# A second layer's attention scores as three rounds of 32-row products, side by side in four banks

## The chip, the cores and the metric

The kernel runs on one core of one Trainium2 chip. The metric is the time of one execution on the device in microseconds (us). The core has five engines that run beside each other, each through its own instructions in order: TensorE (PE: matrix products, with weight loads shown as PEld), VectorE (DVE), ScalarE (ACT), GpSimd (POOL) and SyncE (SP, which only issues DMAs). TensorE writes its results to PSUM, eight banks of 512 float32 per partition; ScalarE and VectorE read them from there.

## The reference

Two attention layers and two gated layers, interleaved, with the same weights both times. One sequence of 2048 tokens, width 448, 16 query heads of 28 with one shared key and value head, and a gated width of 1792:

```
q = (x @ wq) in 16 heads;  k = x @ wk;  v = x @ wv          # x is layer-normalised
p = softmax(q k^T * 28 ** -0.5);  x = x + (p v, heads joined) @ wo
h = sigmoid(x @ w_gate) * (x @ w_up);  x = x + h @ w_down   # x is layer-normalised
```

These two lines of work make one layer of the kernel; there are two layers.

## The kernel before

Precision comes from splitting each float32 into a high and a low float16 part: a product is high by high plus low by high plus high by low. Tokens go in 16 units of 128 queries; keys in 16 tiles of 128 (`kt`). A step is one unit against one tile of keys, so a layer has 256 steps; the four groups of four heads (`g`) are its four score products.

The keys are stored transposed in `KK` with two halves. In the first half the rows are four blocks of 32: low, high, high, high; in the second half four copies of high (built in `kv`, turned in `kvt` or by a DMA). A query tile `QS` holds three blocks of 32 rows: high, high, low. So one product of 96 rows gives all three terms of a score (`scores`, line 584). Row 28 of the first block of `QS` holds the negated, scaled row maximum, and the key tile a constant there, so that the maximum is subtracted within the product. The exp (line 587) empties the bank into `P`.

The maxima come from an earlier pass over the high parts alone (`Maxima.step`, lines 529 to 563): a set of four `mx` products of 32 rows each, one per head, in four row groups of the array and into four banks, each emptied by a maximum on VectorE (line 554). The pass runs one unit ahead, one set per step; in the first three units of the second layer most of the sets were done earlier, and the few that remain are spread over 48 steps (`sparse`). When a unit's maxima are complete, `row_max` transposes them and a DMA writes them into `QS`.

`pv` (line 595) multiplies `P` with the values in four column groups, both for one or two steps at a time. Everything else of the layer (query projections `qp`, output `wo`, the gated layer's `gp`, `up`, `dn`) is the fill: `Filler.slice` issues fill matmuls of about a given length. The length is set so that the fill of a layer lasts to the layer's end: each step pair's share (`2 * rate`) is divided by the number of slices in the pair.

The order within a pair of steps is written out by hand in `PATHS`, one string for even `kt` and one for odd: F is a slice of fill, S one score product with its exp, M a set of `mx`, P one step's `pv`, X the issue of due side work. The second layer takes C for units 0 to 2, then D0 for even and D1 for odd units. Its D0 before is

```
"D0": ("FSFXFSSSPPM", "SSFFXSFSFM"),
```

PSUM: one bank is held by `pv`. The other seven (`BANKS`, `NBK`) are shared by `s`, `mx` and all fill tiles. A tile is given a bank when it is issued, in program order, and its first product waits until the bank's former tile has been read.

Of the kernel before, what the change touches and what calls it, by code (L numbers as in the profile page):

```python
# [8 lines left out]
F32 = mybir.dt.float32  # L9
F16 = mybir.dt.float16  # L10
I32 = mybir.dt.int32
AF = mybir.ActivationFunctionType
OP = mybir.AluOpType
# [6 lines left out]
def interleaved_layers_kernel(ctx: ExitStack, tc: tile.TileContext, x, wq, wk, wv, wo, wg, wu, wd, out, layers=2):  # L20
# [6 lines left out]
    nc = tc.nc  # L27
    _, S, D = x.shape
# [13 lines left out]
    wk1 = ctx.enter_context(tc.tile_pool(name="wk1", bufs=2))  # L42
# [316 lines left out]
    ktl = [cst.tile([128, 8, 32], F16, name=f"ktl{i}") for i in range(2)]  # L359
    for t in ktl:  # L360
        nc.vector.memset(t, 0.0)
        nc.vector.memset(t[:, 0, 28:29], 32768.0)
    KK, VV, QH = {}, {}, {}

    def layer_tiles(l):
# [5 lines left out]
    def kv(l, XT, t, kt):  # L371

        p = fps([128, 56], F32, "kv")
        yield from chain(p, lambda a, c, k: WKV[:k, a, c], lambda c, k: XT[:k, c, t * 128:(t + 1) * 128], 40, False)
        kt_ = ktl[kt % 2]

        def build():
            k = p[:, 0:28].rearrange("p (o d) -> p o d", o=1).to_broadcast([128, 7, 28])
            nc.scalar.activation(kt_[:, 1:8, 0:28], k, AF.Copy, scale=2.0 ** -18)
            nc.scalar.activation(VV[l][:, kt, 0:28], p[:, 28:56], AF.Copy, scale=2.0 ** -16)  # L380
            nc.vector.scalar_tensor_tensor(kt_[:, 0, 0:28], p[:, 0:28], 2.0 ** -18, kt_[:, 1, 0:28],
                                           op0=OP.mult, op1=OP.subtract)
        defer(build)
# [54 lines left out]
    def load_qs(l, u):  # L438
        b, t = divmod(u, 4)
        assert QDONE[l, b] == G  # L440
        q = wk1.tile([96, G, 4, 128], F16, name="QS", bufs=2)
        QS[l, u] = q
        for i, part in ((0, 0), (1, 0), (2, 1)):
            for g in range(G):
                nc.sync.dma_start(q[32 * i:32 * i + 32, g],
                                  qd[l % 2][b, g, part, :, t * 128:(t + 1) * 128].rearrange("(h d) n -> d h n", d=32))
# [118 lines left out]
    def row_max(l, u, mp, n):  # L565

        m32 = wk1.tile([128, 16], F32, name="m32")
        m16 = wk1.tile([128, 16], F16, name="m16")
        nc.vector.tensor_reduce(m32, mp.rearrange("p g h k -> p (g h) k")[:, :, :n], axis=AX.X, op=OP.max)
        nc.vector.tensor_scalar(m16, m32, -(2.0 ** -15), None, op0=OP.mult)  # L570

        def fin():
            stored.add(("m", l, u))
            p = fps([16, 128], F16, "mt")
            nc.tensor.transpose(p, m16, id16)
            r = wk1.tile([16, 128], F16, name="mr")
            nc.vector.tensor_copy(r, p)
            (nc.gpsimd if l or u else nc.sync).dma_start(QS[l, u][28:29].rearrange("o g h n -> o (g h) n"), r)
        late.append([4 if l and u in AHEAD else LT, fin, (l, u)])

    def scores(l, u, kt, g, P):
        assert ("m", l, u) in stored, (l, u, kt)
        s = psf.tile([128, 512], F32, tag=BANKS["s"], name="s", bufs=NBK[BANKS["s"]])
        nc.tensor.matmul(s, KK[l][0:96, 0, kt * 128:(kt + 1) * 128], QS[l, u][:, g].rearrange("p h n -> p (h n)"),  # L584
                         start=True, stop=True)
        p = wk1.tile([128, 512], F32, tag="P", name="P", bufs=12)
        nc.scalar.activation(p, s, AF.Exp, scale=esc)  # L587
        P.append(p)
# [259 lines left out]
    class Filler:  # L848
# [15 lines left out]
        def slice(self, ns):  # L864
            now[0] += 1
            flush()
            self.debt += ns
            for _ in range(3):
                c = next(self.first[0], None) if self.first else None
                if c is None:  # L870
                    self.first[:1] = []
                    break
                self.debt -= c
            while self.gens and self.debt > 0:
                g = self.gens[0]
                c = next(g[0], None)
                if c is None:
                    self.gens.remove(g)
                    continue
                self.debt -= c  # L880
                g[1] -= c
            if not self.gens:
                self.debt = min(self.debt, 0.0)
# [148 lines left out]
    for b in range(1, NB):  # L1032
# [8 lines left out]
        "A": ("FSFSFSFSPXM", "FSFSFSFSPXM"),  # L1041
        "B0": ("FSSFSXSPPM", "SFFSSFFSXMF"),
        "B1": ("FFSSXFSFSPMP", "SSFSFXSFM"),
        "C": ("FFSFXSSSPPM", "FSFXSSFSFM"),
        "D0": ("FSFXFSSSPPM", "SSFFXSFSFM"),
        "D1": ("FSFSXFSSPPM", "SSFFSXFSFM"),
    }

    def pair_of(l, u):
# [9 lines left out]
    for l in range(layers):  # L1059
        mx = mxs[l]  # L1060
        final = l + 1 == layers
        while late:
            late.pop(0)[1]()
        if not l:
            mx.step()
            fill.slice(0.4 * QCH)
            mx.step()
        else:
            mx.todo.sort()
            n = sum(a[0] < 4 for a in mx.todo) + 4  # L1070
            sparse = [i * (3 * KT - 1) // n for i in range(n)]
        if not final:
            layer_tiles(l + 1)
        if l:
            for b in range(2, NB):
                fill.add(qgen(l, b), G * QCH)
        flush(True)
        fill.slice((0.50 if l else 0.4) * QCH)
        waiting = []
        rate = 0.0  # L1080
        for step in range(U * KT):
            u, kt = divmod(step, KT)
            if step == HEAD and not final:
                mxs[l + 1] = Maxima(l + 1)
            P = []
            pair = pair_of(l, u)
            single = "P" in pair[0] and "P" in pair[1]
            for o in pair[kt % 2]:
                if o == "S":
                    scores(l, u, kt, len(P), P)  # L1090
                elif o == "M":
                    if l and step < 3 * KT:
                        n = step in sparse
                    else:
                        n = 1 + (u == 0 and kt in MORE)
                    if not n:
                        mx.visit()
                    for _ in range(n):
                        if not mx.step() and not final and l + 1 in mxs:
                            a = mxs[l + 1].between()  # L1100
                            if a and soon(a[0], mxs[l + 1].need(a)):
                                mxs[l + 1].step(a)
                    if kt == 2 and u + 1 < U:
                        load_qs(l, u + 1)
                elif o == "P":
                    for _ in range(len(waiting) if single else min(1, len(waiting))):
                        pv(*waiting.pop(0))
                elif o == "X":
                    if u and kt == 1:
                        b = (u - 1) // TB  # L1110
                        if (l, b) not in BLK:
                            BLK[l, b] = Block(l, b)
                        later(*BLK[l, b].tile(u - 1))
                    if l == 0:
                        paced(step)
                    tick()
                    fed = sum(BLK[l, b].fed == TB for b in range(NBL) if (l, b) in BLK)
                    if fed < NBL - 1:
                        rate = fill.left / max(FIRST + TB * KT * fed - step, 1)
                    else:  # L1120
                        rate = max(fill.left - KEEP, 0) / (U * KT - step)
                else:
                    fill.slice(2 * rate / "".join(pair).count("F"))
            waiting.append((l, u, kt, P))
        while waiting:
            pv(*waiting.pop(0))
        flush(True)
        later(*BLK[l, NBL - 1].tile(U - 1))
        n = 0
        nx = None if final else mxs[l + 1]  # L1130
        while side or pend or (fill.gens if final else not nx.started()):
            tick()
            for _ in range(0 if fine else 2):
                fill.slice(VS / 2)
            n += 1
            a = None if final else nx.between()
            if a:
                kz = nx.need(a)
                if soon(a[0], kz):
                    go = n >= 2 and not fine  # L1140
                elif kz == S - 128:
                    go = len(fine) > 1
                else:
                    go = True
                if go:
                    nx.step(a)
                    n = 0
            for _ in range(4 if fine else 0):
                fill.slice(VS / 4)
        if not final:  # L1150
            fill.slice(QCH)
# [21 lines left out]
```

## Time and profile before

| | us |
|---|---|
| median of 2 runs | 2256.29 (2255.59 to 2256.99) |
| the profiled execution | 2255.21 |
| its span, first to last instruction | 2253.2 |
| scores of the first layer, first to last | 87.6 to 1106.3 |
| scores of the second layer, first to last | 1226.2 to 2165.8 |
| mean granted TensorE clock | 0.997 of full |

Rows of groups read: line, engine, operation, out<-in, shapes, count, then busy time and mean ns of one, then the engine's idle time ahead of them and what ended it. Rows of a timeline read: start, length, engine, line, what, and in brackets idle time ahead. Matmuls are pipelined, so the length of one is longer than the distance to the next start, and it is the distances that count. In the profile a `pv` product in float32 shows as two instructions.

### The profile page before, as it was taken

What the parts mean: (1) busy time and instruction counts of PE and PEld (TensorE: products, weight loads), DVE (VectorE), ACT (ScalarE), POOL (GpSimd) and SP (SyncE); (2) the same over time, 40 slices, a digit from 0 to 9 for tenths busy, and PEclk for the clock granted to TensorE, in tenths of its full rate; (3) what the DMA queues carried; (4) which work ended last, traced back from release to release, by engine and by line L of the source; (5) the groups of instructions that cost most, each with busy time, mean ns of one, the idle gap of its engine ahead of it and who ended that gap; (6) DMA issues with size and microseconds to landing.
All of it is one profiled execution on the core that took longest, in us unless ns stands there. A gap on an engine that the chain in (4) does not pass through costs nothing.

```text
span 2253.2 us, 41480 instructions
## 1 busy us (share of the span) xinstructions
PE 2200.9 (98%) x15915; PEld 1029.9 (46%) x15915; DVE 1640.0 (73%) x2905; ACT 1546.2 (69%) x2595; POOL 337.5 (15%) x590
## 2 busy tenths in 40 slices
PE   8999999999999999999998999999999999999999
PEld 3322344444544444454563324445454544445467
DVE  7988887877777787777786557777777877777322
ACT  5798776776667677676514997777676767777741
POOL 5114773101110110001011011000000000000010
PEclk9999999999999999999999999999999999999999
DMA  4333662423313142332441123233231323223233
GB/s 142 106 110 92 205 214 59 118 66 89 113 60 103 56 113 76 98 106 56 129 135 35 36 64 97 77 88 98 67 102 56 93 64 102 76 88 96 70 110 119
DMA packets 203622, 213.28 MB, mean 95 GB/s; under 512 B 135376, under 2 KB 164240, under 8 KB 203424
## 3 DMA queue, kind: packets, MB, share of 16 engines
q1 hardware_dynamic: 198080, 195.78, 29.1%
q0 software_dynamic: 5344, 14.87, 1.9%
q8 instruction: 124, 2.03, 0.4%
q14 instruction: 74, 0.61, 0.1%
HBM read 175.37 MB, written 23.59 MB: 88 GB/s over the span
## 4 chain that ended last, share of the span: by engine, by line
PE 86%; DVE 7%; ACT 2%; DMA 2%; issue 1%; POOL 1%; SPq 1%; DVEq 0%; ACTq 0%; POOLq 0%
PE pv L595 20%; PE s L584 19%; PE up L352 12%; PE gp L352 11%; PE dn L784 11%; PE mx L549 7%; DVE mp L554 5%; PE wo L695 3%; PE qp L352 2%; ACT P L587 1%; DMA rgu<-in_B_w_up_dram 0%; DMA sums<-rc 0%; DMA rq<-in_A_wq_dram 0%; PE hot L916 0%; DVE sgu L131 0%
## 5 line engine op out<-in xcount | busy, mean ns | idle before, releaser
L587 ACT ACTIVATE P<-s,esc 128x512 f32<-128x512 f32 x2048 | 1295.5, 690 | 483.3 <-PE s L584 470.7
L554 DVE TENSOR_REDUCE mp<-mx 128x1 f32<-128x512 f32 x2048 | 1270.0, 683 | 394.6 <-PE mx L549 390.3
L584 PE MATMUL s<-QS,KK 96*128 96x512 f16 x2048 | 684.1, 381 | 20.0 <-DVE mp L554 12.6
L352 PEld LDWEIGHTS <-wgu 128*128 128x128 f16 x4928 | 467.6, 97 | 191.2 <-issue 49.6
L595 PE MATMUL pv<-P,VV 128*32 128x512 f32 x4096 | 509.0, 600 | 0.0
L352 PE MATMUL gp<-XT,wgu 128*128 128x256 f16 x2464 | 349.4, 272 | 0.9 <-DVE mp L554 0.7
L352 PE MATMUL up<-XT,wgu 128*128 128x256 f16 x2464 | 346.0, 272 | 1.9 <-DVE mp L554 1.2
L784 PE MATMUL dn<-WD,h 128*128 128x448 f16 x1344 | 298.5, 352 | 0.0
L584 PEld LDWEIGHTS <-KK 96*128 96x128 f16 x2048 | 186.6, 98 | 200.0 <-issue 113.0
L595 PEld LDWEIGHTS pv<-P,VV 128*32 128x32 f32 x4096 | 98.6, 108 | 239.0 <-issue 236.9
L549 PE MATMUL mx<-KK,QH 32*128 32x512 f16 x1792 | 187.5, 385 | 4.0 <-DVE mp L554 2.0
L784 PEld LDWEIGHTS <-h 128*128 128x128 f16 x1344 | 127.0, 97 | 131.6 <-issue 13.5
L549 PEld LDWEIGHTS <-QH 32*128 32x128 f16 x1792 | 46.1, 91 | 257.8 <-issue 253.9
L669 POOL TENSOR_TENSOR lb<-pvs,lb 128x512 f32<-128x512 f32 x32 | 40.4, 1264 | 728.1 <-DMA lb<-sums 647.9
L352 PE MATMUL qp<-XT,WQ 128*128 128x512 f16 x352 | 115.0, 394 | 1.1 <-DVE mp L554 0.4
L754 DVE SCALAR_TENSOR_TENSOR th<-th,up 128x512 f32<-128x512 f32 x112 | 76.3, 682 | 49.0 <-PE up L352 43.5
L306 POOL TENSOR_SCALAR rs<-mv 128x1 f32<-128x1 f32 (+1 forms) x50 | 11.2, 225 | 672.6 <-DVE mv L291 604.1
L757 ACT ACTIVATE h<-th 128x512 f16<-128x512 f32 x112 | 70.5, 629 | 52.7 <-DVE th L754 52.6
L746 ACT ACTIVATE th<-gp,gsc 128x512 f32<-128x512 f32 x112 | 77.1, 688 | 37.8 <-PE gp L352 37.5
L758 DVE SCALAR_TENSOR_TENSOR h<-th,h 128x512 f16<-128x512 f32 x112 | 76.9, 687 | 21.7 <-ACT h L757 21.7
L695 PE MATMUL wo<-WO,oT 128*128 128x448 f16 x384 | 90.7, 353 | 0.2 <-ACT P L587 0.2
L352 PEld LDWEIGHTS <-WQ 128*128 128x128 f16 x352 | 34.0, 100 | 59.6 <-issue 36.0
(151 smaller groups left out, 915.5 us busy)
## 6 DMA issues: line engine op xcount, KB each, us to landing
wgu<-wgu_d SPq DMA_DIRECT2D x224, 512.0 KB
QS<-qd SPq DMA_DIRECT2D x384, 32.0 KB
lb<-sums SPq DMA_DIRECT2D x128, 64.0 KB
xr<-in_A_x_dram SPq DMA_DIRECT2D x32, 224.0 KB
qd<-qst POOLq DMA_DIRECT2D x28, 256.0 KB, 2.7
wgu_d<-sgu POOLq DMA_DIRECT2D x14, 512.0 KB, 3.7
x2d<-x SPq DMA_DIRECT2D x16, 224.0 KB
xr<-x2d SPq DMA_DIRECT2D x16, 224.0 KB
```

What stands on the lines that cost most here:

```text
L352: nc.tensor.matmul(ps, a, b, start=n == 0, stop=n == 10)
L549: nc.tensor.matmul(ps[h][:, i * w:(i + 1) * w], qh[32 * h:32 * h + 32, g], KK[l][32 * h:32 * h + 32, 1, ka:kz], start=True, stop=True, til ...
L554: nc.vector.tensor_reduce(o, ps[h].rearrange("p (g k) -> p g k", g=n), axis=AX.X, op=OP.max)
L584: nc.tensor.matmul(s, KK[l][0:96, 0, kt * 128:(kt + 1) * 128], QS[l, u][:, g].rearrange("p h n -> p (h n)"), start=True, stop=True)
L587: nc.scalar.activation(p, s, AF.Exp, scale=esc)
L595: nc.tensor.matmul(v[32 * g:32 * g + 32], VV[l][:, kt], P[g], start=kt == 0, stop=kt == KT - 1, tile_position=(0, 32 * g))
L695: nc.tensor.matmul(p, v["oT"][:, a, h * 128:(h + 1) * 128], WO[:, c, h], start=n == 0, stop=n == 11)
L746: defer(lambda: nc.scalar.activation(th, gp.rearrange("p j n -> p (j n)"), AF.Tanh, scale=gsc))
L754: nc.vector.scalar_tensor_tensor(t, th, 1.0, up.rearrange("p j n -> p (j n)"), op0=OP.add, op1=OP.mult)
L757: nc.scalar.activation(h[:, 0], t, AF.Copy, scale=2.0 ** -17)
L758: defer(lambda: nc.vector.scalar_tensor_tensor(h[:, 1], t, 2.0 ** -17, h[:, 0], op0=OP.mult, op1=OP.subtract), 2)
L784: nc.tensor.matmul(p, hs[f // 2][:, a, o:o + 128], WD[:, f, c], start=n == 0, stop=n == 3 * FC - 1)
```

## The change

In the second layer only, the four score products of a step become one block (`Y` in the paths). Key rows now hold four copies of low in the first half of `KK` and four of high in the second. A query tile holds head group `g` in rows 32g to 32g+31, its high part and its low part behind each other. `block` takes four banks and issues twelve products of 32 rows and 512 columns in three rounds: low key by high query, high by high, high by low, each round with the four groups in four row groups of the array, each group adding in its own bank. The four exps follow. The maxima go to `QS` by four DMAs instead of one, the query tile is loaded by eight DMAs instead of twelve, and one `mx` set fewer is spread over the first three units (`+ 3` for `+ 4`).

```diff
-        nc.vector.memset(t[:, 0, 28:29], 32768.0)
+        nc.vector.memset(t[:, 0:4, 28:29], 32768.0)
...
-            nc.scalar.activation(kt_[:, 1:8, 0:28], k, AF.Copy, scale=2.0 ** -18)
+            nc.scalar.activation(kt_[:, 4 if l else 1:8, 0:28], k[:, 0:4] if l else k, AF.Copy, scale=2.0 ** -18)
             nc.scalar.activation(VV[l][:, kt, 0:28], p[:, 28:56], AF.Copy, scale=2.0 ** -16)
+            if l:
+                nc.vector.scalar_tensor_tensor(kt_[:, 0:4, 0:28], k[:, 0:4], 2.0 ** -18, kt_[:, 4:8, 0:28],
+                                               op0=OP.mult, op1=OP.subtract)
+                return
...
-        q = wk1.tile([96, G, 4, 128], F16, name="QS", bufs=2)
+        q = wk1.tile([128, G, 4, 128], F16, name="QS", bufs=2)
         QS[l, u] = q
+        if l:
+            for i in range(2):
+                for g in range(G):
+                    nc.sync.dma_start(q[32 * g:32 * g + 32, i],
+                                      qd[l % 2][b, g, i, :, t * 128:(t + 1) * 128].rearrange("(h d) n -> d h n", d=32))
+            return
...
+            if l:
+                for g in range(G):
+                    nc.gpsimd.dma_start(QS[l, u][32 * g + 28:32 * g + 29, 0], r[4 * g:4 * g + 4])
+                return
...
+    def block(l, u, kt, P):
+        assert ("m", l, u) in stored, (l, u, kt)
+        q, k = QS[l, u].rearrange("p i h n -> p i (h n)"), KK[l][:, :, kt * 128:(kt + 1) * 128]
+        s = [psf.tile([128, 512], F32, tag=BANKS["s"], name="s", bufs=NBK[BANKS["s"]]) for _ in range(G)]
+        for n, (a, c) in enumerate(((0, 0), (1, 0), (1, 1))):
+            for g in range(G):
+                r = slice(32 * g, 32 * g + 32)
+                nc.tensor.matmul(s[g], k[r, a], q[r, c], start=n == 0, stop=n == 2, tile_position=(32 * g, 0))
+        for g in range(G):
+            p = wk1.tile([128, 512], F32, tag="P", name="P", bufs=12)
+            nc.scalar.activation(p, s[g], AF.Exp, scale=esc)
+            P.append(p)
...
-        "C": ("FFSFXSSSPPM", "FSFXSSFSFM"),
-        "D0": ("FSFXFSSSPPM", "SSFFXSFSFM"),
-        "D1": ("FSFSXFSSPPM", "SSFFSXFSFM"),
+        "C": ("FXFFYPPMF", "FXFYFFFM"),
+        "D0": ("FFFXYPPMFF", "FYFFXFM"),
+        "D1": ("FFXFFYPPM", "FFFXYFFFM"),
...
-            n = sum(a[0] < 4 for a in mx.todo) + 4
+            n = sum(a[0] < 4 for a in mx.todo) + 3
...
-                if o == "S":
+                if o == "Y":
+                    block(l, u, kt, P)
+                elif o == "S":
```

What this does to the order is seen at three places. First, TensorE in the middle of the second layer, at the end of an even step. Before, the last three scores, `pv` and a set of `mx` stand there; the names in brackets are the counters waited for, of VectorE (DVE_49) and of ScalarE (Activation_49), which show who must have emptied the bank.

```order
L584 MATMUL s<-QS,KK 128x512 [waits DVE_49]
L584 LDWEIGHTS KK
L584 MATMUL s<-QS,KK 128x512 [waits DVE_49]
L595 MATMUL pv<-P,VV 32x512 x8
L549 LDWEIGHTS QH
L549 MATMUL mx<-KK,QH 128x512 [waits Activation_49]
L549 LDWEIGHTS QH
L549 MATMUL mx<-KK,QH 128x512 [waits DVE_49]
L549 LDWEIGHTS QH
L549 MATMUL mx<-KK,QH 128x512 [waits Activation_49]
L549 LDWEIGHTS QH
L549 MATMUL mx<-KK,QH 128x512 [waits DVE_49]
```

The same place now, from the last two products of the block's third round on:

```order
L602 MATMUL s<-QS,KK 128x512
L602 LDWEIGHTS KK
L602 MATMUL s<-QS,KK 128x512
L622 MATMUL pv<-P,VV 32x512 x8
L559 LDWEIGHTS QH
L559 MATMUL mx<-KK,QH 128x512 [waits DVE_49]
L559 LDWEIGHTS QH
L559 MATMUL mx<-KK,QH 128x512 [waits DVE_49]
L559 LDWEIGHTS QH
L559 MATMUL mx<-KK,QH 128x512 [waits Activation_49]
L559 LDWEIGHTS QH
L559 MATMUL mx<-KK,QH 128x512 [waits Activation_49]
```

The two banks that the set takes from ScalarE are now banks of the block that stands right ahead of it. Second, TensorE at the beginning of a step. Before, single scores stand between pieces of fill (here the output product `wo`), after a set of `mx`:

```order
L549 LDWEIGHTS QH
L549 MATMUL mx<-KK,QH 128x512 [waits Activation_49]
L695 LDWEIGHTS oT
L695 MATMUL wo<-WO,oT 128x448
L695 LDWEIGHTS oT
L695 MATMUL wo<-WO,oT 128x448
L695 LDWEIGHTS oT
L695 MATMUL wo<-WO,oT 128x448
L584 LDWEIGHTS KK
L584 MATMUL s<-QS,KK 128x512 [waits Activation_49]
```

Now the whole first round of the block stands there, after ten matmuls of fill (the last is shown) that follow the set of `mx`:

```order
L352 LDWEIGHTS wgu
L352 MATMUL up<-XT_20843,wgu 128x256
L602 LDWEIGHTS KK
L602 MATMUL s<-QS,KK 128x512 [waits Activation_49]
L602 LDWEIGHTS KK [waits PE_49]
L602 MATMUL s<-QS,KK 128x512 [waits Activation_49]
L602 LDWEIGHTS KK
L602 MATMUL s<-QS,KK 128x512 [waits DVE_49]
L602 LDWEIGHTS KK
L602 MATMUL s<-QS,KK 128x512 [waits DVE_49]
L602 LDWEIGHTS KK
L602 MATMUL s<-QS,KK 128x512
```

The block's last two banks are those of the first two products of the `mx` set ahead of it. Third, ScalarE in the second layer. Before, `th` and `h` of the gated layer stand between exps of one to three scores:

```order
L587 ACTIVATE P<-s,esc 128x512 [waits PE_49]
L587 ACTIVATE P<-s,esc 128x512 [waits PE_49,Activation_49] x2
L587 ACTIVATE P<-s,esc 128x512 [waits PE_49] x2
L746 ACTIVATE th<-gp,gsc 128x512 [waits PE_49]
L587 ACTIVATE P<-s,esc 128x512 [waits PE_49,Activation_49]
L587 ACTIVATE P<-s,esc 128x512 [waits PE_49] x3
L587 ACTIVATE P<-s,esc 128x512 [waits PE_49,Activation_49]
```

Now exps stand in runs of four, and `th` and `h` between blocks:

```order
L773 ACTIVATE th<-gp,gsc 128x512 [waits PE_49]
L605 ACTIVATE P<-s,esc 128x512 [waits PE_49,Activation_49] x8
L784 ACTIVATE h<-th 128x512 [waits DVE_49]
L773 ACTIVATE th<-gp,gsc 128x512 [waits PE_49]
L605 ACTIVATE P<-s,esc 128x512 [waits PE_49,Activation_49] x8
```

The count of exps and of maxima is the same as before.

More of the change, by code (lines that the diff above doesn't have):

```diff
@@ L583, in scores @@
         s = psf.tile([128, 512], F32, tag=BANKS["s"], name="s", bufs=NBK[BANKS["s"]])
-        nc.tensor.matmul(s, KK[l][0:96, 0, kt * 128:(kt + 1) * 128], QS[l, u][:, g].rearrange("p h n -> p (h n)"),
+        nc.tensor.matmul(s, KK[l][0:96, 0, kt * 128:(kt + 1) * 128], QS[l, u][0:96, g].rearrange("p h n -> p (h n)"),
                          start=True, stop=True)
```

## The prediction

> **What bounds the kernel now.** I read the page first: busy time of each engine, then the chain that ended last.
>
> ```profile
> PE 2200.9 (98%) x15915; PEld 1029.9 (46%) x15915; DVE 1640.0 (73%) x2905; ACT 1546.2 (69%) x2595; POOL 337.5 (15%) x590
> ...
> PE 86%; DVE 7%; ACT 2%; DMA 2%; issue 1%; POOL 1%; SPq 1%; DVEq 0%; ACTq 0%; POOLq 0%
> ...
> L587 ACT ACTIVATE P<-s,esc 128x512 f32<-128x512 f32 x2048 | 1295.5, 690 | 483.3 <-PE s L584 470.7
> L554 DVE TENSOR_REDUCE mp<-mx 128x1 f32<-128x512 f32 x2048 | 1270.0, 683 | 394.6 <-PE mx L549 390.3
> L584 PE MATMUL s<-QS,KK 96*128 96x512 f16 x2048 | 684.1, 381 | 20.0 <-DVE mp L554 12.6
> ```
>
> TensorE is never idle for long and is 86% of the chain. The other two large consumers empty its PSUM banks: ScalarE takes an exp from each score bank, VectorE a maximum from each `mx` bank. They wait for TensorE (470.7 and 390.3 us), while the scores wait for banks for only 20.0 us in the whole run. Next, the second layer alone by windows:
>
> ```profile
> 1226.20:2165.80 939.60, 933.73 (x6713) 429.93 (x6714) 646.40 (x1105) 712.25 (x1152) 74.54 (x158) 1.00 0.26 79
> ...
> 1500.00:1650.00 150.00, 149.62 (x1112) 71.88 (x1109) 114.98 (x196) 109.02 (x174) 10.81 (x23) 1.00 0.27 83
> ```
>
> The columns are the length, then busy time of PE, PEld, DVE, ACT, POOL, then granted clock. PE is busy 149.6 of 150 us at full clock, while DVE and ACT have a quarter of their time left. On this reading less PE work is a shorter layer, as long as banks keep coming free. So I read two steps in order of time, PE first, then ACT and DVE.
>
> ```profile
> 1500.22 0.40 PE L549 MATMUL mx<-KK,QH 32*128 32x512 f16 x4
> 1500.55 0.61 PE L584 MATMUL s<-QS,KK 96*128 96x512 f16 x2
> 1500.99 1.04 PE L352 MATMUL gp<-XT,wgu 128*128 128x256 f16 x8
> 1501.87 0.38 PE L584 MATMUL s<-QS,KK 96*128 96x512 f16 x1
> 1502.09 0.60 PE L352 MATMUL gp<-XT,wgu 128*128 128x256 f16 x4
> 1502.52 0.38 PE L584 MATMUL s<-QS,KK 96*128 96x512 f16 x1
> 1502.74 0.60 PE L352 MATMUL gp<-XT,wgu 128*128 128x256 f16 x4
> 1503.28 0.40 PE L549 MATMUL mx<-KK,QH 32*128 32x512 f16 x4
> 1503.60 0.61 PE L352 MATMUL gp<-XT,wgu 128*128 128x256 f16 x4
> 1504.05 0.38 PE L584 MATMUL s<-QS,KK 96*128 96x512 f16 x1
> 1504.27 0.27 PE L352 MATMUL gp<-XT,wgu 128*128 128x256 f16 x1
> 1504.38 0.49 PE L352 MATMUL up<-XT,wgu 128*128 128x256 f16 x3
> 1504.71 0.38 PE L584 MATMUL s<-QS,KK 96*128 96x512 f16 x1
> 1504.93 0.60 PE L352 MATMUL up<-XT,wgu 128*128 128x256 f16 x4
> 1505.36 0.60 PE L584 MATMUL s<-QS,KK 96*128 96x512 f16 x2
> 1505.89 1.92 PE L595 MATMUL pv<-P,VV 128*32 128x512 f32 x16
> 1507.75 0.39 PE L549 MATMUL mx<-KK,QH 32*128 32x512 f16 x4
> ```
>
> ```profile
> 1504.47 0.69 ACT L587 ACTIVATE P<-s,esc 128x512 f32<-128x512 f32 x1 [0.34 <-PE s L584]
> 1505.05 0.68 ACT L746 ACTIVATE th<-gp,gsc 128x512 f32<-128x512 f32 x1
> 1505.62 1.84 ACT L587 ACTIVATE P<-s,esc 128x512 f32<-128x512 f32 x3
> ```
>
> ```profile
> 1500.64 2.48 DVE L554 TENSOR_REDUCE mp<-mx 128x1 f32<-128x512 f32 x4 [1.39 <-PE mx L549]
> ```
>
> From one start to the next this prices everything. A pair of steps is 1500.22 to 1507.75, 7.53 us. A score product is (1500.99 - 1500.55) / 2 = 0.22, a fill matmul (1501.87 - 1500.99) / 8 = 0.11, and the pair holds 28 of them, 3.08 us. Changing how the array is split costs: the four fill matmuls ahead of `mx` take 0.54 instead of 0.44, so entering row groups is 0.10; the two scores ahead of `pv` take 0.53, so entering column groups is 0.09; the two `pv` take 1.86 with leaving. A set of four `mx` holds the array 0.33 before the next work starts. How much of that is leaving, and whether further rounds in the same row groups need their weights waited for, is shown where sets were cut into narrower products:
>
> ```profile
> 1212.73 0.40 PE L549 MATMUL mx<-KK,QHB 32*128 32x128 f16 x16
> 1213.07 1.11 PE L352 MATMUL qp<-XT,WQ 128*128 128x512 f16 x3
> ...
> 1173.33 0.40 PE L549 MATMUL mx<-KK,QHB 32*128 32x256 f16 x8
> 1173.66 0.72 PE L352 MATMUL up<-XT,wgu 128*128 128x256 f16 x5
> ```
>
> Four rounds of 128 columns (0.34), two of 256 (0.33) and one of 512 (0.33) hold the array equally long. So rounds follow each other at the pace of their columns, weight loads hidden: a round of 512 is 0.22, leaving is 0.11.
>
> For the banks: an exp starts 0.42 after its product (1504.05 to 1504.47), a first maximum 0.42 after its `mx` (1500.22 to 1500.64). Three exps run in 1.84, so (1.84 - 0.69) / 2 = 0.575 apart; four maxima in 2.48, so (2.48 - 0.68) / 3 = 0.60 apart. After the last round of four products that end together, the second and third bank are free at 0.42 + 0.575 + 0.69 = 1.69 and 2.26; after a set of `mx`, at 0.42 + 0.60 + 0.68 = 1.70 and 2.30.
>
> **Part 1: the products themselves.** Per step four scores of 0.22 (0.88) become three rounds of 0.22 (0.66): -0.44 per pair. In the even step, entering and leaving row groups (0.21) replaces entering `pv` from full width (0.09): +0.12. In the odd step both are new: +0.21. Net -0.11 per pair, and 128 pairs give **-14 us**. Leaving row groups straight into `pv` is not in the trace; I take the 0.11 seen towards full width. Between nothing and twice that, the term moves 14 us either way.
>
> **Part 2: when the banks come free.** Scores, `mx` and fill share seven banks. Before, the score products are spread over the step and each has its exp behind it within about 0.4 us. Now a block needs four banks at once, and none has its result until the third round; then four exps queue. A block, a set of `mx` and one or two fill tiles make nine or ten tiles for seven banks, so each set takes two or three banks from the set just before it. I counted this from the banks that the built program assigns: of 210 times that `mx` follows a block, the last bank needed is the second exp's 165 times and the third's 45 times; of 211 blocks after `mx`, the second maximum's 143 times and the third's 68 times. The waits in the order above say the same: two of four wait for ScalarE, two for VectorE.
>
> What lies between is too short. A pair has 3.08 us of fill in nine slices (units 0 to 2 and even units) or eleven (odd ones): 0.34 or 0.28 each. From the start of a set's last round to the next set is 0.22 + 0.11 + the slices + 0.10:
> - odd step, block to `mx`: three slices, 1.45 or 1.27, mean 1.36. Short of 1.69 by 0.33, of 2.26 by 0.90; weighted 79 to 21: 0.45.
> - even step, block to `mx`: 0.22 + 0.11 + 1.86 = 2.19; short only of 2.26: 0.02.
> - even step's `mx` to the next block: three slices, 1.36; short of 1.70 by 0.34, of 2.30 by 0.94; weighted 68 to 32: 0.53.
> - odd step's `mx` to the next block: 1.5, plus what `mx` itself waited (its first two products run at once and their maxima go ahead): at least 1.83, short only of 2.30: 0.13.
>
> Together 1.13 us per pair in which TensorE stands, with fill, `pv` and all else queued behind it in order. About 210 steps have a set of `mx` (the first three units have few, the last none), so 105 pairs: **+119 us**. The waits that are there now are too few to return much: they are in the 20.0 us above.
>
> **Part 3: other work in the two queues.** `th` (row 1505.05) and `h` stand between the exps, `th` and `h` again between the maxima, 56 each in this layer. Hidden now; one in four ahead of a needed bank, half of it (0.3) exposed, is 224 / 4 x 0.3 = **+17 us**, an estimate from those rows, with 0 and 60 as ends.
>
> **Part 4: what is hidden.** Query loads go from twelve to eight per unit; SyncE needs 5.73 us for twelve and loads a unit ahead, so fewer gain nothing. The row of maxima goes in four DMAs on GpSimd, not one:
>
> ```profile
> 1678.56 5.73 SPq L445 DMA_DIRECT2D QS<-qd  x12
> ```
>
> ```profile
> L578 POOL DMA_DIRECT2D QS<-mr x31: 522/606/637, 136.4 to 2100.7; - x31
> ...
> DMA to landing us min/median/max: 1.6/1.7/5.2
> ```
>
> Four issues of 0.61 and 1.7 to land are 4.1 us, 1.8 more. One sparse `mx` set fewer lets them start three steps ahead of the unit instead of four; two steps, 7.4 us, remain after the transpose. Without that cover it is under 2 us for each of 15 units. The low key part is now built four times, 16 times in all:
>
> ```profile
> L381 DVE SCALAR_TENSOR_TENSOR ktl<-kv,ktl x32: 174/184/189, 18.8 to 1216.9; 128x28 f16<-128x28 f32 x32
> ```
>
> At most four times 0.18, so 0 to 9 us on VectorE, between the layers, mostly beside fill; I take nothing, as ScalarE's copy ahead of it shrinks.
>
> **Sum.** -14 + 119 + 17 = +122. The profiled execution took 2255.2 us, 1.1 under the median of the runs, so 2256.3 + 122 = 2378 us.
>
> **Rivals.**
> 1. *Banks in time* (the other side). If exps and maxima keep ahead, only part 1 is left: 2242, and 2222 with the 20.0 us of waits gone too. It holds if a block and its `mx` are 1.69 us apart, 0.33 more than counted. For it: both engines have a quarter of their time left. Against: it isn't their load but four results ending together. Over 2% faster (under 2211) would need the mode changes to be free as well: 0.44 x 128 = 56 us, 2200.
> 2. *Rounds dearer than their columns.* If weights of a row group cannot load while it computes, two further rounds a step each wait for a load, 98 ns:
>
> ```profile
> L584 PEld LDWEIGHTS <-KK 96*128 96x128 f16 x2048 | 186.6, 98 | 200.0 <-issue 113.0
> ```
>
> That is 0.20 x 256 = +51, 2429. Against it are the rows with 16 and 8 products. The Trainium skill ("TensorE: Matmul & The Clock Gate", Part 3 on packing small matmuls) says that a weight load overlaps matmuls in flight only where the row group differs, and gives 3.07x for four row groups at 512 columns. By that ratio a round is 0.88 / 3.07 = 0.29, an estimate from that page: 0.86 per block, part 1 becomes +37 and the sum again 2429. This case's trace does not agree: 0.33 with one, two or four rounds.
> 3. *Waits relieve each other.* A wait at `mx` gives the maxima and fill evictions time, so only half of part 2 is left: -14 + 60 = 2302; a little more relief is within 2%.
> 4. *Not side by side.* If products into four banks with sums run one after another, a block is 12 x 0.22 = 2.64: +1.76 x 256 = 450, 2706. `mx` already runs four row groups into four banks, though without adding.
>
> **Chances.** Forecast 0.70; rival 1: 0.11 (0.03 of it under 2211); rival 2: 0.09; rival 3: 0.08; rival 4: 0.02. A measurement tells about 2%, 45 us. Range: from rival 3's 2300 to 2440, which takes in rival 2, part 3's upper end and part 1's. Slower by over 2% are the forecast, rivals 2 and 4 and half of rival 3: 0.85; faster 0.03; within 0.12.
>
> **What would show it.** Right: idle time of PE ahead of `s` and `mx` in the second layer of some 130 us, ended by VectorE's maxima for `s` and by the exps for `mx`; the layer's windows showing PE at about 90% instead of 99.7%; a block's three rounds holding the array 0.66 and 0.1 for each change. Wrong: sets of `mx` that start on time in odd steps, a block over 0.9 us without a wait, or waits on GpSimd's DMAs at a unit's start. The first layer should be unchanged.

## The result and the profile after

The changed kernel takes 2373.8 us (2373.19 to 2374.41, 2 runs) against 2256.29: a ratio of 1.0523, 95% interval 1.0497 to 1.0549. It is 5% slower. The page of the changed kernel, with the engines, the chain of waits, and the groups of the block's products, the `mx` sets, and the first layer's scores:

```profile
PE 2288.7 (97%) x17963; PEld 1008.5 (43%) x17963; DVE 1643.3 (69%) x2905; ACT 1519.6 (64%) x2595; POOL 362.5 (15%) x638
...
PE 79%; DVE 10%; ACT 5%; issue 3%; DMA 1%; POOL 1%; SPq 0%; ACTq 0%; DVEq 0%; POOLq 0%
...
L611 PE MATMUL s<-QS,KK 96*128 96x512 f16 x1024 | 348.7, 381 | 17.1 <-DVE mp L564 11.1
...
L602 PE MATMUL s<-QS,KK 32*128 32x512 f16 x3072 | 291.1, 381 | 24.6 <-DVE mp L564 16.8
...
L559 PE MATMUL mx<-KK,QH 32*128 32x512 f16 x1792 | 209.9, 384 | 9.1 <-ACT P L605 4.3
```

At first sight TensorE is as busy as before, 97% against 98%, and idle ahead of the blocks for only 24.6 us. The chain tells more: TensorE's share fell from 86% to 79%, and VectorE and ScalarE together went from 9% to 15%. The view of the scores gives first and last start of each layer's products:

```profile
L602 PE MATMUL s<-QS,KK x3072: 371/374/630, 1231.0 to 2282.8; 32*128 32x512 f16 x192
L611 PE MATMUL s<-QS,KK x1024: 376/381/634, 89.0 to 1110.4; 96*128 96x512 f16 x171
```

The first layer takes 1021.4 us (1018.7 before), the second 1051.8 instead of 939.6. So 112.2 of the 118.2 us by which the span grew lie in the second layer's 256 steps. A pair of its steps in order of time, PE and then DVE and ACT:

```profile
1704.20 0.39 PE L559 MATMUL mx<-KK,QH 32*128 32x512 f16 x4
1704.53 1.05 PE L352 MATMUL up<-XT,wgu 128*128 128x256 f16 x8
1705.50 1.26 PE L602 MATMUL s<-QS,KK 32*128 32x512 f16 x12
1706.70 1.16 PE L352 MATMUL up<-XT,wgu 128*128 128x256 f16 x9
1707.79 0.57 PE L559 MATMUL mx<-KK,QH 32*128 32x512 f16 x4
1708.29 0.50 PE L352 MATMUL up<-XT,wgu 128*128 128x256 f16 x3
1708.62 1.15 PE L352 MATMUL gp<-XT,wgu 128*128 128x256 f16 x9
1709.70 1.25 PE L602 MATMUL s<-QS,KK 32*128 32x512 f16 x12
1710.88 1.92 PE L622 MATMUL pv<-P,VV 128*32 128x512 f32 x16
1712.74 0.39 PE L559 MATMUL mx<-KK,QH 32*128 32x512 f16 x4
```

```profile
1704.62 2.48 DVE L564 TENSOR_REDUCE mp<-mx 128x1 f32<-128x512 f32 x4 [1.87 <-PE mx L559]
1708.21 2.48 DVE L564 TENSOR_REDUCE mp<-mx 128x1 f32<-128x512 f32 x4 [1.10 <-PE mx L559]
```

```profile
1706.67 2.42 ACT L605 ACTIVATE P<-s,esc 128x512 f32<-128x512 f32 x4 [1.94 <-PE s L602]
1708.96 0.63 ACT L702 CAST oT<-lb 128x512 f16<-128x512 f32 x1
1710.85 2.42 ACT L605 ACTIVATE P<-s,esc 128x512 f32<-128x512 f32 x4 [1.26 <-PE s L602]
```

The pair takes 1704.20 to 1712.74, 8.54 us against 7.53. A block that waits for nothing holds the array 0.76 us, from its first start to the next work's (all 16 blocks of the last unit, which has no sets of `mx`). Here the two blocks hold it 1706.70 - 1705.50 = 1.20 and 1.18, and the odd step's `mx` holds it 1708.29 - 1707.79 = 0.50 instead of 0.33. The wait stands inside the set: the first products start at once, the last one or two when their banks are free, and the next rounds queue behind them. With 1704.20 as the start of `mx` and maxima from 1704.62, the second maximum ends at 1704.62 + 0.60 + 0.68 = 1705.90; the fourth product of the block starts at 1705.96 in the trace. The second block needs the third maximum of the next set, which ends at 1708.21 + 2 x 0.60 + 0.68 = 1710.09; its fourth product starts at 1710.15 in the trace.

This holds beyond one pair. I laid the banks that the built program assigns beside the trace: of 223 sets and blocks in units 3 to 14 that wait more than 0.05 us, 220 start their fourth product 0.05 to 0.11 us after an exp or a maximum has emptied one of their four banks, the last one to come free.

As the wait stands inside the set, the page hardly shows it as idle time: a product's record is 0.37 to 0.39 us long, and the three that started keep the engine busy on paper. So below I give, from the starts of all second-layer matmuls of a trace, the time from the first to the fourth product of each block and set, summed. Unhindered it is 0.01 us. A block counts as even when `pv` follows it, a set when `pv` stands ahead of it. "Rest" is the layer's length (first to last score product) without these waits.

| run | second layer | blocks, odd step | blocks, even | `mx`, odd | `mx`, even | sum of waits | rest |
|---|---|---|---|---|---|---|---|
| changed kernel | 1051.8 | 57.1 | 48.7 | 38.6 | 3.1 | 147.5 | 904 |
| maxima halved | 995.8 | 14.6 | 22.9 | 51.3 | 2.3 | 91.1 | 905 |
| exps halved | 1021.7 | 59.3 | 50.5 | 10.3 | 1.1 | 121.2 | 901 |
| both halved | 948.3 | 16.5 | 14.2 | 14.5 | 1.1 | 46.2 | 902 |
| six banks | 1200.7 | 110.9 | 63.0 | 87.4 | 12.3 | 273.5 | 927 |
| one round | 935.2 | 55.0 | 47.8 | 24.5 | 3.6 | 130.9 | 804 |

In the kernel before, the `mx` sets' sum is 3.8 us and its scores are single products.

### The profile page after: what moved, and what is told of

It reads as the page before. It is cut to its first block, busy times and chain, and to the rows that moved or that the text cites. A ratio compares the mean times of both kernels' runs of the same rounds, so it can differ in the third digit from the quotient of the medians.

```text
span 2371.4 us, 46157 instructions
## 1 busy us (share of the span) xinstructions
PE 2288.7 (97%) x17963; PEld 1008.5 (43%) x17963; DVE 1643.3 (69%) x2905; ACT 1519.6 (64%) x2595; POOL 362.5 (15%) x638
## 4 chain that ended last, share of the span: by engine, by line
PE 79%; DVE 10%; ACT 5%; issue 3%; DMA 1%; POOL 1%; SPq 0%; ACTq 0%; DVEq 0%; POOLq 0%
PE pv L622 19%; PE up L352 10%; PE gp L352 10%; PE dn L811 10%; PE s L602 9%; PE s L611 9%; DVE mp L564 8%; PE mx L559 7%; ACT P L605 3%; PE wo L722 3%; PE qp L352 2%; ACT P L614 1%; DVE sgu L131 0%; DMA sums<-rc 0%; DMA rq<-in_A_wq_dram 0%
## 5 line engine op out<-in xcount | busy, mean ns | idle before, releaser
L605 ACT ACTIVATE P<-s,esc 128x512 f32<-128x512 f32 x1024 | 618.8, 689 | 365.2 <-PE s L602 364.9
L614 ACT ACTIVATE P<-s,esc 128x512 f32<-128x512 f32 x1024 | 644.2, 691 | 262.7 <-PE s L611 259.3
L352 PEld LDWEIGHTS <-wgu 128*128 128x128 f16 x4928 | 457.3, 98 | 207.8 <-issue 113.7
L611 PE MATMUL s<-QS,KK 96*128 96x512 f16 x1024 | 348.7, 381 | 17.1 <-DVE mp L564 11.1
L352 PE MATMUL gp<-XT,wgu 128*128 128x256 f16 x2464 | 335.4, 273 | 1.1 <-DVE mp L564 0.7
L352 PE MATMUL up<-XT,wgu 128*128 128x256 f16 x2464 | 332.4, 273 | 0.9 <-ACT P L614 0.9
L602 PE MATMUL s<-QS,KK 32*128 32x512 f16 x3072 | 291.1, 381 | 24.6 <-DVE mp L564 16.8
L811 PE MATMUL dn<-WD,h 128*128 128x448 f16 x1344 | 291.3, 353 | 0.0
L559 PE MATMUL mx<-KK,QH 32*128 32x512 f16 x1792 | 209.9, 384 | 9.1 <-ACT P L605 4.3
L602 PEld LDWEIGHTS <-KK 32*128 32x128 f16 x3072 | 81.4, 92 | 180.1 <-issue 146.2
L611 PEld LDWEIGHTS <-KK 96*128 96x128 f16 x1024 | 95.7, 98 | 111.0 <-issue 70.3
L306 POOL TENSOR_SCALAR rs<-mv 128x1 f32<-128x1 f32 (+1 forms) x50 | 11.3, 226 | 747.6 <-DVE mv L291 740.3
L784 ACT ACTIVATE h<-th 128x512 f16<-128x512 f32 x112 | 71.2, 636 | 57.1 <-DVE th L781 57.0
L773 ACT ACTIVATE th<-gp,gsc 128x512 f32<-128x512 f32 x112 | 77.7, 694 | 41.7 <-PE gp L352 41.4
```

The costliest lines, as they stand in the source:

```text
L352: nc.tensor.matmul(ps, a, b, start=n == 0, stop=n == 10)
L559: nc.tensor.matmul(ps[h][:, i * w:(i + 1) * w], qh[32 * h:32 * h + 32, g], KK[l][32 * h:32 * h + 32, 1, ka:kz], start=True, stop=True, til ...
L602: nc.tensor.matmul(s[g], k[r, a], q[r, c], start=n == 0, stop=n == 2, tile_position=(32 * g, 0))
L605: nc.scalar.activation(p, s[g], AF.Exp, scale=esc)
L773: defer(lambda: nc.scalar.activation(th, gp.rearrange("p j n -> p (j n)"), AF.Tanh, scale=gsc))
L784: nc.scalar.activation(h[:, 0], t, AF.Copy, scale=2.0 ** -17)
```

## The experiments

Four experiments have a ratio, from four to ten runs; the other five are one run each. Runs of the kernel before, repeated beside them, lie between 2254.98 and 2263.35 us.

**Four full-height products in the block's place.** The kernel before with the new places of work:

```diff
-        "D0": ("FSFXFSSSPPM", "SSFFXSFSFM"),
+        "D0": ("FFFXSSSSPPMFF", "FSSSSFFXFM"),
...
-            n = sum(a[0] < 4 for a in mx.todo) + 4
+            n = sum(a[0] < 4 for a in mx.todo) + 3
```

> The kernel before with the new order of work: where the new paths have a block, four score products of 96 rows stand one after another (0.88 us), all else as before. Theory (banks are late because the four results of a block end together): here the first exp starts 0.66 us ahead of the fourth product, so counted from the last product the second bank is free after 1.03 us instead of 1.69, and the last product of the four comes 0.66 us later for the maxima. Sets of mx should hardly wait, products wait only for a third maximum (about 0.1 us per pair): 2256 to 2285 us. Rival (the places of the work in the step are at fault, whatever the products): it stays within 20 us of 2374. Rival (32-row rounds or changes of the array's split are dear): 2256, no waits.

Measured 2285.35 us, ratio 1.0119 (1.0097 to 1.0141): at the upper edge of the theory's range, and 88 us below the changed kernel. Its second layer takes 968.7 us. Sets of `mx` wait 16.5 us in sum, and single products wait more than I expected, for maxima. In order of time:

```profile
1643.15 0.60 PE L352 MATMUL gp<-XT,wgu 128*128 128x256 f16 x4
1643.59 0.82 PE L584 MATMUL s<-QS,KK 96*128 96x512 f16 x3
1644.63 0.38 PE L584 MATMUL s<-QS,KK 96*128 96x512 f16 x1 [0.22 <-DVE mp L554]
1644.85 1.04 PE L352 MATMUL gp<-XT,wgu 128*128 128x256 f16 x8
1645.81 0.40 PE L549 MATMUL mx<-KK,QH 32*128 32x512 f16 x4
```

The fourth product should start 0.66 us after the first, at 1644.25; it starts at 1644.63. So the places alone cost 29 us of the 118, and the form of the products, with results that end together, costs the other 88 or so. The rival that blames the places alone, with a time near 2374, falls; a quarter of the loss is theirs all the same.

**Maxima halved.** Of the changed kernel, the second layer's maxima read half of each bank:

```diff
-                nc.vector.tensor_reduce(o, ps[h].rearrange("p (g k) -> p g k", g=n), axis=AX.X, op=OP.max)
+                src = ps[h].rearrange("p (g k) -> p g k", g=n)
+                nc.vector.tensor_reduce(o, src[:, :, 0:w // 2] if l else src, axis=AX.X, op=OP.max)
```

> The changed kernel, but in the second layer each maximum reads only half of the columns of its bank (leaves out half of the keys in the maxima). A maximum should take about 0.36 us instead of 0.68. Theory (banks): the second and third maximum end 1.1 and 1.4 us after their set, under the 1.36 us that lie between, so blocks in steps with a set ahead stop waiting (their waits sum to about 63 us in the steady units of the changed kernel), while sets of mx wait as before or more (26 us there), and blocks of the first three units, which wait for exps, keep theirs: 2285 to 2325 us. Rival (array: rounds and changes of split are dear): within 10 us of 2374. Rival (ScalarE's load is the limit): within 20 us of 2374.

Measured 2305.84 us, in the theory's range; neither rival fits. Groups of its maxima, whole and halved:

```profile
L565 DVE TENSOR_REDUCE mp<-mx 128x1 f32<-128x512 f32 x1024 | 634.0, 682 | 153.4 <-PE mx L559 151.0
L565 DVE TENSOR_REDUCE mp<-mx 128x1 f32<-128x256 f32 x1008 | 358.8, 417 | 512.8 <-PE mx L559 510.8
```

With 417 ns instead of 682 the blocks' waits fall from 105.8 to 37.5 us, and those of `mx` rise from 41.7 to 53.7. I take the rise to come from blocks that no longer wait and so end sooner before the set, while the exps take as long as before.

**Exps halved.** The other side; `pv` reads the half twice and costs TensorE the same:

```diff
-            nc.scalar.activation(p, s[g], AF.Exp, scale=esc)
+            nc.scalar.activation(p[:, 0:256], s[g][:, 0:256], AF.Exp, scale=esc)
...
+            x = P[g][:, 0:256].rearrange("p (o n) -> p o n", o=1).to_broadcast([128, 2, 256]) if l else P[g]
...
```

> The changed kernel, but in the second layer each exp reads and writes only half of its bank, and pv reads that half twice, so that TensorE has the same work (leaves out half of the queries' scores). An exp should take about 0.36 us. Theory (banks): sets of mx in odd steps stop waiting (26 us in the steady units, 13 us in the first three), blocks of the first three units, which wait for exps, too (about 40 us); blocks in steady units still wait for maxima, a little more than now (63 to 85 us): 2290 to 2325 us. Rival (array): within 10 us of 2374. Rival (VectorE's load is the limit): within 30 us of 2374.

Measured 2339.99 us, 15 us above the range. The waits of `mx` go as expected (41.7 to 11.3 us), and the blocks' waits in units 3 to 14 grow (70.7 to 82.8 us). What I had wrong were the first three units: their blocks' waits only fall from 35.0 to 26.8 us. I had taken them for waits for exps, but in the changed kernel the delays within these blocks end 17.3 us with an exp and 16.9 us with a maximum; here it is 6.6 and 19.6 us. The chains of this run and of the one before it, in the middle of the second layer, show what each halving leaves (first this run, with halved exps):

```profile
by line: PE pv L623 21.7%; PE s L602 20.5%; DVE mp L564 14.2%; PE dn L812 11.1%; PE up L352 10.1%; PE gp L352 8.5%; PE mx L559 8.3%; PE wo L723 3.0%; issue 1.9%; PE mt L585 0.2%; DVE h L786 0.2%; ACT P L605 0.2%; DVE oT L704 0.1%; ACT h L78
```

The run with halved maxima:

```profile
by line: PE pv L623 22.5%; PE s L603 19.9%; PE up L352 12.5%; PE gp L352 11.8%; PE dn L812 11.5%; PE mx L559 9.7%; ACT P L606 5.8%; PE wo L723 3.3%; issue 2.5%; ACTq L606 0.2%; DVE h L786 0.1%; ACT h L785 0.1%; DVE mp L565 0.0%; ACTq L703 0
```

The maxima (`mp`) stand at 14.2% and 0.0%, the exps (`P`) at 0.2% and 5.8%. In the changed kernel they are 9.9% and 5.0%, in the kernel before the maxima are 1.9% and the exps under 0.1%:

```profile
by line: PE pv L622 21.4%; PE s L602 20.3%; DVE mp L564 9.9%; PE up L352 9.8%; PE gp L352 9.7%; PE dn L811 9.0%; PE mx L559 8.5%; ACT P L605 5.0%; issue 3.4%; PE wo L722 2.5%; DVE h L785 0.2%; ACTq L605 0.1%; DVE oT L703 0.1%; ACT h L784 0.
```

```profile
by line: PE pv L595 23.7%; PE s L584 22.6%; PE gp L352 14.0%; PE up L352 14.0%; PE dn L784 11.8%; PE mx L549 8.3%; PE wo L695 2.7%; DVE mp L554 1.9%; issue 0.5%; PE qp L352 0.4%; PE mt L575 0.1%
```

**Both halved, in both kernels.** The edits above together, in the changed kernel and, with the same meaning, in the kernel before.

> The changed kernel with both halvings in the second layer: maxima read half of a bank, exps read and write half of it, pv reads that half twice (leaves out half of the keys in the maxima and half of the scores). TensorE's work and order are those of the changed kernel. Theory (banks): with 0.42 us maxima and 0.48 us exps the second and third bank are free within 1.36 us, so nearly all of the 147 us of waits in blocks and sets go, and what is left is the products: 2235 to 2255 us, within 15 us of the kernel before with the same two halvings. Rival (array: rounds or changes of split cost more than counted): 2270 us or more, and over 20 us above the kernel before with the halvings.

> The kernel before with the same two halvings in its second layer (leaves out the same parts). Its scores hardly wait for banks there, so it should gain only the 15 to 23 us of small waits of its second layer: 2232 to 2245 us. The difference to the changed kernel with the halvings is what the products alone bring: -14 us was predicted, -20 to +10 expected here, as some waits of the first three units may stay. If the engines' load had been the limit of the kernel before, it would fall by more than 40 us.

Measured 2262.15 us for the changed kernel so altered, ratio to the kernel before 1.0016 (1.0007 to 1.0026), and 2236.37 for the kernel before so altered, 0.9898 (0.988 to 0.9916). The second is in its range, and as it gains only some 20 us, the load of VectorE and ScalarE was not what held the kernel before. The first is 7 us over its own range, and 26 us over the second where I expected 10 at most. That meets one of the two signs that I had named for dear rounds (over 20 us above), not the other (2270 or more). The table says what the 26 us are: 46.2 us of waits are left, 25.8 of them in the first 220 us of the layer. Where nothing waits, the products are cheaper as counted; in order of time:

```profile
1643.05 0.83 PE L603 MATMUL s<-QS,KK 32*128 32x512 f16 x12
1643.80 1.16 PE L352 MATMUL up<-XT,wgu 128*128 128x256 f16 x9
1644.89 0.40 PE L559 MATMUL mx<-KK,QH 32*128 32x512 f16 x4
1645.22 0.50 PE L352 MATMUL up<-XT,wgu 128*128 128x256 f16 x3
```

The block holds the array 0.75 us here with its exit, and `mx` 0.33. The second layer of the kernel before with the halvings is 926.5 us; some 10 us of that, an estimate good to a few us, is time by which starts come later than usual for their kind, which leaves some 916. The changed kernel's "rest" is 901 to 905 in four runs. So the products and changes of split alone bring about 12 us, and the rival that called them dear falls by the "rest" and the 0.75 us of a block, although the time came nearer to its bound than I expected.

**Six banks instead of seven**, in both kernels:

```diff
-    NBK = {"f": 7, "s": 2, "m": 3}
+    NBK = {"f": 6, "s": 2, "m": 3}
```

> The changed kernel with six shared banks in place of seven. Theory (banks): each set then takes one more bank from the set just ahead of it, one more exp (0.575 us) or maximum (0.60 us): the four waits of a pair grow by some 1.6 us together, 105 pairs: 2500 to 2580 us. Rival (array, or the order of work): under 2400 us. The first layer's and the time between the layers grow as they do in the kernel before with six banks.

> The kernel before with six shared banks in place of seven. Theory: its single scores free their banks one by one, so the lost bank costs its second layer much less than it costs the changed kernel's: under 60 us in the second layer against 120 us or more there; the whole 2290 to 2390 us. Rival (both kernels live off the seventh bank alike): the same loss in both second layers.

Measured 2603.97 and 2420.95 us, both above their ranges. The first layer, equal in both, loses 80.2 and 75.8 us, which I had left too small in both expectations. The second layer loses 148.9 us in the changed kernel (1051.8 to 1200.7) and 84.8 in the kernel before (939.6 to 1024.4), where I expected under 60. The direction is the theory's, the ratio smaller than I had it: the kernel before also lives off its seventh bank. In the changed kernel 126 of the 149 us are in the sets and blocks: 273.5 us of waits instead of 147.5. The other 23 are in the "rest", and may be the clock: it was granted at 0.50 for 60 us of this layer, against 14 us in the changed kernel, which is worth up to (60 - 14) / 2 = 23 us.

**One round only.** Two of the three rounds left out:

```diff
-        for n, (a, c) in enumerate(((0, 0), (1, 0), (1, 1))):
+        for n, (a, c) in enumerate(((0, 0),)):
```

> The changed kernel with only the first of the three rounds of a block (leaves out two of the three terms of the second layer's scores). Theory (banks): the time from a block's last round to the next set is the same, so the waits stay about as they are (some 145 us in sets and blocks), and the layer is shorter by two rounds, 0.43 x 256 = 110 us: 2250 to 2275 us. Rival (rounds are dearer than 0.215 us each, weights not loaded ahead): a fall of 130 us or more, to 2244 or less. Rival (the engines' load per step sets the pace): waits grow by what the rounds give, and the time stays over 2330 us.

Measured 2252.25 us, in the theory's range. The rest of the layer falls by 904 - 804 = 100 us, 0.20 us for each of 512 rounds left out, and a block of the last unit holds the array 0.33 us instead of 0.76, 0.215 per round. One score product of the same 512 columns holds it 0.22 in the kernel before, so a further round is not dearer than its columns. The waits stay near: 130.9 instead of 147.5.

**The same work spread evenly.** The changed kernel with other places in units 3 to 15:

```diff
-        "D0": ("FFFXYPPMFF", "FYFFXFM"),
-        "D1": ("FFXFFYPPM", "FFFXYFFFM"),
+        "D0": ("FFFFXYPFMPF", "YFFXFFM"),
+        "D1": ("FFFFXYPFMPF", "YFFXFFM"),
```

> The changed kernel with the same work put in other places in units 3 to 15 of the second layer: even step FFFFXYPFMPF, odd step YFFXFFM, so that all four distances between a block and a set are about 1.67 us instead of 1.36, 2.19, 1.36 and 1.5, for one more entry into and exit from column groups per pair (0.21 us). Theory (distance against 1.69 and 1.70 us for a second bank, 2.3 for a third): a pair's waits fall from 1.05 to about 0.7 us, mostly for a third bank: 105 pairs x (0.21 - 0.4), some -15 to -25 us: 2345 to 2360 us. Rival (the number of banks held is the limit, wherever the work stands): within 8 us of 2374 or more. Rival (changes of split are dear): over 2390 us.

Measured 2385.02 us, ratio 1.0565 (1.0548 to 1.0583): 11 us slower than the changed kernel, where I expected 15 to 25 faster; of the rivals, the one that calls the number of banks the limit wherever the work stands fits. Its second layer takes 1064.6 us. The odd step's blocks do stop waiting (57.1 to 20.6 us), but sets of `mx` wait 62.7 instead of 41.7, and the even blocks 50.2 instead of 48.7. In units 3 to 14 the even blocks still wait for a third maximum in 43 of 96 steps. The sum only falls from 147.5 to 133.5, and the rest grows by 931 - 904 = 27 us, near the 22 us that the additional exit and entry of column groups should cost (0.21 in each of 104 pairs); up to 4 more may be the clock, granted at 0.50 for 21 us against 14. In order of time, a block that now waits 0.72 us for its fourth bank, and a split of `pv`:

```profile
1703.13 0.50 PE L602 MATMUL s<-QS,KK 32*128 32x512 f16 x3
1703.85 0.80 PE L602 MATMUL s<-QS,KK 32*128 32x512 f16 x9 [0.23 <-DVE mp L564]
1704.59 1.06 PE L622 MATMUL pv<-P,VV 128*32 128x512 f32 x8
1705.59 0.50 PE L352 MATMUL up<-XT,wgu 128*128 128x256 f16 x3
1706.02 0.39 PE L559 MATMUL mx<-KK,QH 32*128 32x512 f16 x4
1706.34 1.06 PE L622 MATMUL pv<-P,VV 128*32 128x512 f32 x8
```

So a wait removed in one place mostly came back in the next. No version here that does the whole work beats the kernel before.

## Why the prediction was right, and where it was not

The sign, the mechanism and the size came out: 2373.8 against 2378. That the size came so near is in part luck, as terms that were too large and too small made up for each other. By its steps:

- **Products (-14 us).** Right, within what can be told. "Rest" is 904 us. The kernel before has some 916, by its halved run as by its own trace (939.6 less some 23 us of late starts), which makes -12, an estimate good to a few us, and up to -18 if the slower clock below is taken off. The last unit, which has no sets of `mx`, shows the gain undisturbed: 52.4 us instead of 54.2.
- **Banks (+119).** The mechanism is right, the sizes are only near. I divided the fill of a pair of odd units by eleven slices; their path has ten, so the distances are a little longer, and the same sum gives some 110. Per pair in units 3 to 14, odd `mx` was 0.45 and measured 0.30, even `mx` 0.02 and 0.03, the odd step's block 0.53 and 0.43, the even step's block 0.13 and 0.30. The last is the term most off: I took it that the wait of `mx` in the odd step would nearly always cover it. In 40 of 96 steps this block waits for the third maximum, 0.61 us each; the set ahead of it had waited only 0.18 us on average there, not 0.33.
- **Other work in the queues (+17).** The runs don't show it. In units 3 to 14 other work (`h`) stands ahead of the exp or maximum that decides in 3 of the 220 waits above, 3.0 us together.
- **Waits of before.** I called them too few to return much. But some 23 us of late starts in the second layer of before are gone, so the 147.5 us of new waits are 124 net, against 119 + 17 = 136.
- **Where in the layer.** Two errors cancelled here. Units 3 to 14 lose 83 us (756.1 to 838.9), 0.86 per pair where the steps gave 1.18 (their waits are 102 us, 1.06 per pair, less the gain in products and the small waits that were there before). The first three units lose 31 (129.3 to 160.6), though I had priced few of their steps: their waits sum to 45 us. A little of it is the clock, which the sum leaves out: the granted clock in these units is 0.97 on average, against 1.00 before. In the whole layer it is 0.50 for 14 us (1233.4 to 1240.2, for one) and for 1 us before, which is worth 7 us at most; why it falls there, no run shows. There the fill is a few query projections, so a block follows `mx` or another block sooner. In the changed kernel:

```profile
1274.71 0.39 PE L352 MATMUL qp<-XT,WQ 128*128 128x512 f16 x1
1275.04 0.89 PE L602 MATMUL s<-QS,KK 32*128 32x512 f16 x3
1276.15 0.80 PE L602 MATMUL s<-QS,KK 32*128 32x512 f16 x9 [0.23 <-DVE mp L564]
1276.89 0.60 PE L352 MATMUL qp<-XT,WQ 128*128 128x512 f16 x2
1277.43 0.54 PE L602 MATMUL s<-QS,KK 32*128 32x512 f16 x3
1278.17 0.80 PE L602 MATMUL s<-QS,KK 32*128 32x512 f16 x9 [0.21 <-ACT P L605]
```

  The first block's fourth product comes 1.11 us late, behind maxima, the second's 0.74 us, behind the exps of the block ahead of it.
- **What would show it.** Half wrong. A block and the changes of split are as named: 0.76 us with its exit. But I named idle time of TensorE of some 130 us and windows at 90%. The page has 24.6 and 9.1 us, and the layer's PE is 97% busy. The waits are there, but within sets, under records of products that already started. The chain and the distances between starts show them.
- **What is hidden.** Right: in the view of the scores TensorE waits for a row of maxima to land in `QS` once, 0.7 us (0.4 before).

Rival 1 (banks in time) fell with the result, rival 2 (dear rounds) with the run of one round, and rival 4 with the 0.76 us of a free block. Rival 3, that waits relieve each other, may hold in part: a pair in units 3 to 14 waits 1.06 us and not 1.29. But that gap is also what the slices and the other work come to, so no run shows relief by itself. Some 6 of the 118 us lie outside the second layer, 2.7 of them in the first, and stay unexplained.

## What to carry to other kernels

Before merging products so that several results end together, add up how long each bank is held and how many of the next set's banks come from the set just before: the time between the two sets has to cover that, whatever the engines' load. A gain of 0.22 us per step in products on the busiest engine (56 us), of which the changes of split left some 12, was lost many times over in waits for engines that stand idle a third of the time. And where products overlap, look for waits in the distances between starts and in the chain, not in the busy share.

## What was not expected of the hardware

A halved exp takes 475 ns against 687, and a halved maximum 417 against 682: neither is half. If the time grows evenly with the columns, some 0.15 us (maximum) to 0.26 us (exp) of each does not depend on them. Much of that is hidden when they follow each other: from start to start halved maxima are 0.33 us apart against 0.60, halved exps 0.36 against 0.57. Reading half of a tile twice as the moving operand of `pv` cost TensorE nothing: `pv` for two steps holds the array 1.86 us with it and without it.
